# Attention followed by two dense layers: transposing a stacked query block through a 128-row identity instead of a 64-row one

## The chip, the core and the metric

The kernel runs on one core of one Trainium2 chip. The metric is device time in microseconds (us) for one execution; the median of three runs is given. The engines are named as in the profile: PE is TensorE's matrix multiply, PEld its load of the stationary operand, DVE is VectorE, ACT is ScalarE, POOL is GpSimd, SP is SyncE, which issues the transfers.

## The reference

Causal attention with a decay, over 4 batches of 8 heads, 576 positions of 64 features, followed by two dense two-matrix layers over 2304 tokens (512 to 2048 to 512), the first with a squared ReLU, the second with an ELU:

```python
scores = np.matmul(q, k.T) / sqrt(64) + cum[:, None] - cum[None, :]     # cum = cumsum(log f)
attn   = softmax(where(causal, -1e9, scores)) ; y = attn @ v             # per batch and head
x = y as [2304, 512]
x = relu(x @ w_in)**2 @ w_out
x = elu(x @ w2_in) @ w2_out
```

## The kernel before

Everything is float32. Where the kernel wants the precision and not the slow float32 product, it splits a tensor into a rounded high part and a low remainder (type `F32R`) and multiplies the parts in turn. Batch 0 (`PLAIN`) is not split: its products are plain float32, each recorded as two PE instructions, and its product with V has 64 output rows (`128*64` in the rows: 128 rows in, 64 columns of the stationary operand). Batches 1 to 3 are split; there the product with V carries the high and low part of V side by side and has 128 columns.

Per head the 576 queries are cut into five blocks of rows: blocks 0 and 1 (step "A"), blocks 2 and 3 (step "B"), and the last 64 queries (step "4"). A block of only 64 rows would fill half of the 128 partitions, so step "4" stacks the last 64 queries of two heads: head 0 of the pair in partitions 0 to 63, head 1 in 64 to 127. The stacked tile of probabilities is `e4` (`e4s`, 128 x 640; columns 576 to 639 are zero).

To multiply probabilities with V, they have to be transposed, since V's product contracts over keys. `tr` (L376 to L378) is a PE instruction: the probabilities are the stationary operand, an identity matrix is the moving one, and the transposed block lands in a PSUM tile `pt`. In `out_b` the inner function `turn(J)` does this for the 128 keys number J: for J = 0, 1, 2 one block from `e4`, and two from the head's own tile `e`; for J = 3 two blocks from `e4` (keys 384 to 511, and the last 64 keys) and one from `e`. Because `e4` holds two heads, the kernel takes only this head's half of the partitions, `e4[p, j]` with `p` the 64 partitions of head `k`, and a 64 x 64 piece of the identity. Those instructions have the shape `64*128 64x64` in the rows; the others are `128*128 128x128`. After a turn, ACT (L373) copies `pt` to a rounded tile and DVE (L374) makes the remainder (in batch 0 one copy, by ACT or DVE), and `av` (L379 to L385) multiplies. For the last 64 keys (J = 4) `av` is called with `rows=64`: it contracts over 64 partitions for 64 queries, again an instruction of 64 rows.

Between the instructions of the attention, the PE works on pieces of the first layer ("units", L157, tiles `ph` and `o`), which are put in by a credit scheme. The order of instructions on each engine is fixed before the run by the framework, which plays through a timeline of its own with modelled costs; the PE takes them strictly in that order. After the attention the remaining units run, and then the rest of the first layer and the second layer, nearly all of it L157.

The lines that the change touches: the identity (L96, L97), `tr`, `av`, and in `out_b` the functions `unsplit` and `turn` and the call of `av` for J = 4.

Of the kernel before, what the change touches and what calls it, by code (L numbers as in the profile page):

```python
# [10 lines left out]
F32 = mybir.dt.float32  # L11
# [33 lines left out]
CP = {'pA': 'a', 'pB': 'av', 'xA': 'a', 'xB': 'a'}  # L45
# [19 lines left out]
def f32(ap):  # L65
    return ap.bitcast(F32)
# [10 lines left out]
def attention_then_moe_kernel(ctx, tc, first, firstv, plain, qkv, aug0, f, w1, w2, out):  # L77
    nc = tc.nc
    PS = bass.MemoryType.PSUM

    def pool(stack, name, bufs, side, **kw):
        return stack.enter_context(tc.tile_pool(name=name, bufs=bufs, side=side, reuse_waits="tile", **kw))

    const = pool(ctx, "const", 1, "left")
# [8 lines left out]
    blocks = [(t0, min(512, NT - t0)) for t0 in range(0, NT, 512)]  # L93
    x2 = [dram.tile([2 * NC, 128, n], F32, name=f"x2_{j}") for j, (t0, n) in enumerate(blocks)]

    ident = const.tile([128, 128], F32, name="ident")  # L96
    make_identity(nc, ident)  # L97

    def mask(ap, pat):
        nc.gpsimd.affine_select(out=ap, in_=ap, pattern=pat, compare_op=ALU.is_ge, fill=-8.0e9, base=0, channel_multiplier=1)  # L100
# [3 lines left out]
    seen = [None]  # L104
# [8 lines left out]
    def copy(eng, dst, x, scale=None):  # L113
        if eng == "a":
            nc.scalar.activation(out=dst, in_=x, func=AF.Copy, scale=1.0 if scale is None else scale)  # L115
        elif eng == "p":
            nc.gpsimd.tensor_scalar(dst, x, 1.0 if scale is None else scale, 0.0, op0=ALU.mult, op1=ALU.add)
        elif scale is None:
            nc.vector.tensor_copy(dst, x)
        else:  # L120
            nc.vector.tensor_scalar(dst, x, scale, None, op0=ALU.mult)
# [250 lines left out]
    def split_pt(pt, hi, lo):  # L372
        nc.scalar.activation(out=hi, in_=pt, func=AF.Copy)  # L373
        nc.vector.tensor_tensor(lo, pt, f32(hi), op=ALU.subtract)  # L374

    def tr(dst, src, p0=0):  # L376
        k = src.shape[0]
        seen[0] = nc.tensor.transpose(dst, src, ident[p0:p0 + k, p0:p0 + k])  # L378

    def av(dst, hh, J, hl, first, last, rows=128):  # L380
        if isinstance(hh, Plain):
            seen[0] = nc.tensor.matmul(out=dst[0:64], lhsT=hh.v[0:rows, J, :], rhs=hl[0], start=first, stop=last)  # L382
            return
        for i in range(2):
            seen[0] = nc.tensor.matmul(out=dst, lhsT=hh[2][0:rows, J, :], rhs=hl[i], start=first and i == 0, stop=last and i == 1)  # L385

    def fold(pv, n, x, c0, k, eng, hh=None):
        if isinstance(hh, Plain):
            copy(eng, x[64 * k:64 * k + 64, c0:c0 + n], pv[0:64, 0:n])
            return  # L390
        t = ab.tile([64, 320], F32, tag="t", name="t", bufs=BUFS["t"])
        nc.scalar.activation(out=t[:, 0:n], in_=pv[64:128, 0:n], func=AF.Copy)
        if eng == "v":
            nc.vector.tensor_tensor(x[64 * k:64 * k + 64, c0:c0 + n], pv[0:64, 0:n], t[:, 0:n], op=ALU.add)
        else:
            u = ab.tile([64, 320], F32, tag="t", name="u", bufs=BUFS["t"])
            nc.scalar.activation(out=u[:, 0:n], in_=pv[0:64, 0:n], func=AF.Copy)
            nc.gpsimd.tensor_tensor(out=x[64 * k:64 * k + 64, c0:c0 + n], in0=u[:, 0:n], in1=t[:, 0:n], op=ALU.add)

    def norm_x(b, hp, kind, x, c0):  # L400
        z = zs.pop((kind, b, hp))
        r = ab.tile([128, 2, 2], F32, tag="r", name="r")
        nc.gpsimd.tensor_scalar(r, z, 1.0, 1e-9, op0=ALU.mult, op1=ALU.add)
        nc.vector.reciprocal(r, r)
        rb = ab.tile([128, 2, 2, 64], F32, tag="rb", name="rb", bufs=1)
        copy("p", rb, r.unsqueeze(3).broadcast_to([128, 2, 2, 64]))
        pr = ps_t.tile([128, 512], F32, tag="t", name="pr")
        for i in range(2):
            tr(pr[:, i * 128:i * 128 + 128], rb[:, i])
        nc.vector.tensor_tensor(x[:, c0:c0 + 256], x[:, c0:c0 + 256], pr[:, 0:256], op=ALU.mult)  # L410
# [12 lines left out]
    def out_a(hh, e, x, k):  # L423
        pt = ps_t.tile([128, 512], F32, tag="t", name="pt")
        tr(pt[:, 0:128], e[:, 0:128])
        tr(pt[:, 128:256], e[:, 256:384])
        tr(pt[:, 256:384], e[:, 128:256])
        if isinstance(hh, Plain):
            copy(CP["pA"], e, pt[:, 0:384])
            yield  # L430
            pv = ps_v.tile([128, 512], F32, tag="v", name="pv")
            av(pv[:, 0:256], hh, 0, [e[:, 0:256]], True, False)
            av(pv[:, 0:128], hh, 1, [e[:, 256:384]], False, True)
            fold(pv, 256, x, 0, k, CP["xA"], hh)
            return
        hl = ptA[k]
        split_pt(pt[:, 0:384], hl[0][:, 0:384], hl[1][:, 0:384])
        yield
        pv = ps_v.tile([128, 512], F32, tag="v", name="pv")
        av(pv[:, 0:256], hh, 0, [t[:, 0:256] for t in hl], True, False)  # L440
        av(pv[:, 0:256], hh, 1, [t[:, 256:512] for t in hl], False, True)
        fold(pv, 256, x, 0, k, FOLD[0])

    def out_b(hh, e, e4, x, k):
        p = slice(64 * k, 64 * k + 64)
        native = isinstance(hh, Plain)

        def unsplit(pt, n, J):
            p = ab.tile([128, 320], F32, tag=f"p{J % 2}", name="pp", bufs=BUFS["p"])
            copy(CP["pB"][J % 2], p[:, 0:n], pt[:, 0:n])  # L450
            return [p]

        def turn(J):
            j = slice(J * 128, J * 128 + 128)
            pt = ps_t.tile([128, 512], F32, tag="t", name="pt")
            if J < 3:
                tr(pt[:, 0:64], e4[p, j], 64 * k)
                tr(pt[:, 64:192], e[:, j])
                tr(pt[:, 192:320], e[:, 512 + J * 128:640 + J * 128])
                if native:  # L460
                    return unsplit(pt, 320, J)
                hl = [ab.tile([128, 320], F32R, tag=f"p{t}", name=f"p{t}", bufs=BUFS["p"]) for t in range(2)]
                split_pt(pt[:, 0:320], hl[0], hl[1])
            else:
                tr(pt[:, 0:64], e4[p, 512:640], 64 * k)
                tr(pt[:, 64:128], e4[p, 384:512], 64 * k)
                tr(pt[:, 128:256], e[:, 384:512])
                if native:
                    return unsplit(pt, 256, J)
                hl = ptB[k]  # L470
                split_pt(pt[:, 0:256], hl[0][:, 0:256], hl[1][:, 0:256])
            return hl

        hls = [turn(0)]
        yield
        hls.append(turn(1))
        yield
        pv = ps_v.tile([128, 512], F32, tag="v", name="pv")
        for J in range(4):
            hl = hls[J]  # L480
            if J < 3:
                av(pv[:, 0:320], hh, J, hl, J == 0, False)
            else:
                n3 = 192 if native else 256
                av(pv[:, 0:n3], hh, 3, [t[:, 64:64 + n3] for t in hl], False, False)
                av(pv[:, 0:64], hh, 4, [t[0:64, 0:64] for t in hl], False, True, 64)
                fold(pv, 320, x, 0, k, CP["xB"] if native else FOLD[1], hh)
            if J < 2:
                hls.append(turn(J + 2))
            yield  # L490

    heads = {}
    e4 = {}
# [16 lines left out]
    def outs(b, hp, kind, k):  # L510
        if kind == "4":
            return
        if k == 0:
            xs[kind] = a1.tile([128, 320], F32, tag="x" + kind, name="x" + kind, bufs=BUFS["x"])
        x = xs[kind]
        e = es.pop((b, hp, kind, k))
        if kind == "A":
            yield from out_a(heads[b, hp, k], e, x, k)
            if k:
                norm_x(b, hp, "A", x, 0)  # L520
                store_x(b, hp, x, 0, 256)
        else:
            yield from out_b(heads[b, hp, k], e, e4[b, hp], x, k)
            if k:
                norm_x(b, hp, "B", x, 64)
                store_x(b, hp, x, 256, 320)
        yield
# [159 lines left out]
    for i in range(len(todo) + LAG):  # L687
# [8 lines left out]
        if i < len(todo):  # L696
            sg = soft(*todo[i])
            b, hp, kind, k = todo[i]
# [215 lines left out]
```

## Time and profile before

| | |
|---|---|
| median of 3 runs | 1086.64 us (1085.25 to 1087.79) |
| the profiled execution | 1085.59 us, its span 1083.7 us |
| PE busy | 1059.4 us, 98% of the span |
| DVE, ACT, POOL busy | 58%, 46%, 21% |
| attention stage | about 13 to 398 us, the rest is the two layers |

Busy time of the PE counts an instruction from its start to its end. Matmuls are pipelined: one begins long before the one ahead of it has ended. So what an instruction costs is read from starts: the time from its start to the start of the next one on the PE. A row of the timeline merges neighbours of the same line, operation and tiles; "x3" is three of them, and its two numbers are the start of the first and the time until the end of the last.

### The profile page before, as it was taken

What the parts mean: (1) busy time and instruction counts of PE and PEld (TensorE: products, weight loads), DVE (VectorE), ACT (ScalarE), POOL (GpSimd) and SP (SyncE); (2) the same over time, 40 slices, a digit from 0 to 9 for tenths busy, and PEclk for the clock granted to TensorE, in tenths of its full rate; (3) what the DMA queues carried; (4) which work ended last, traced back from release to release, by engine and by line L of the source; (5) the groups of instructions that cost most, each with busy time, mean ns of one, the idle gap of its engine ahead of it and who ended that gap; (6) DMA issues with size and microseconds to landing.
All of it is one profiled execution on the core that took longest, in us unless ns stands there. A gap on an engine that the chain in (4) does not pass through costs nothing.

```text
span 1083.7 us, 15458 instructions
## 1 busy us (share of the span) xinstructions
PE 1059.4 (98%) x5696; PEld 875.5 (81%) x5696; DVE 624.0 (58%) x1363; ACT 495.2 (46%) x1055; POOL 228.7 (21%) x260
## 2 busy tenths in 40 slices
PE   3999999999999999999999999999999999999998
PEld 2557678899988998889988888888888888888897
DVE  6684467766677535886876358963433433343343
ACT  4675587876777544444543234532222222222232
POOL 4456387574757230000000000000000000000000
PEclk9999999999999999999999999999999999999999
DMA  8563434435341116444486145500300300110010
GB/s 240 156 198 106 156 127 155 140 95 181 111 151 65 42 64 217 127 140 168 140 288 206 67 155 174 194 21 1 117 1 1 117 1 1 47 32 0 1 40 20
DMA packets 60060, 115.48 MB, mean 107 GB/s; under 512 B 7296, under 2 KB 34688, under 8 KB 59968
## 3 DMA queue, kind: packets, MB, share of 16 engines
q1 hardware_dynamic: 59984, 114.49, 33.1%
q8 instruction: 45, 0.74, 0.3%
q14 instruction: 31, 0.25, 0.1%
HBM read 87.37 MB, written 27.69 MB: 106 GB/s over the span
## 4 chain that ended last, share of the span: by engine, by line
PE 95%; DMA 3%; ACT 1%; POOL 0%; DVE 0%; issue 0%; SPq 0%; ACTq 0%; POOLq 0%; DVEq 0%
PE O L157 31%; PE pH L157 31%; PE pt L378 7%; PE o L157 6%; PE ph L157 6%; PE pv L385 4%; PE pv L382 3%; PE s L305 2%; PE s L309 2%; PE s L310 2%; DMA raws_w<-in_w_dram 1%; PE pr L378 1%; DMA rawA<-ca 1%; DMA xu<-x 0%; DMA x<-xs 0%
## 5 line engine op out<-in xcount | busy, mean ns | idle before, releaser
L157 PE MATMUL pH<-xu,w 128*128 128x512 f32 (+1 forms) x1632 | 354.0, 367 | 0.0
L157 PEld LDWEIGHTS pH<-xu,w 128*128 128x128 f32 x1632 | 282.9, 188 | 55.3
L157 PE MATMUL O<-w,gh 128*128 128x512 f32 x576 | 179.0, 394 | 0.0
L556 ACT ACTIVATE g<-g 128x512 f32<-128x512 f32 (+1 forms) x80 | 47.0, 589 | 197.1 <-DVE g L555 196.9
L157 PEld LDWEIGHTS O<-w,gh 128*128 128x128 f32 x576 | 107.2, 188 | 24.7
L157 PE MATMUL O<-gh,w 128*128 128x512 f32 (+1 forms) x448 | 122.0, 362 | 0.0
L111 DVE TENSOR_TENSOR gl<-g,gh 128x512 fp32r<-128x512 f32 (+1 forms) x136 | 85.2, 627 | 54.2 <-ACT gh L558 44.4
L157 PE MATMUL O<-w,gl 128*128 128x512 f32 x288 | 111.3, 392 | 0.0
L555 DVE TENSOR_SCALAR g<-pH 128x512 f32<-128x512 f32 (+1 forms) x80 | 51.0, 638 | 101.4 <-PE pH L157 101.3
L157 PEld LDWEIGHTS O<-gh,w 128*128 128x128 f32 x448 | 79.8, 189 | 14.2
L124 POOL TENSOR_TENSOR qk<-raw,qk 64x704 fp32r<-64x704 f32 (+1 forms) x48 | 78.3, 1632 | 22.8 <-ACT qk L115 20.2
L157 PE MATMUL O<-gl,w 128*128 128x512 f32 (+1 forms) x224 | 79.4, 363 | 0.0
L557 DVE SCALAR_TENSOR_TENSOR g<-g,pH 128x512 f32<-128x512 f32 (+1 forms) x80 | 50.7, 634 | 46.3 <-ACT g L556 46.0
L157 PE MATMUL o<-gh,w 128*128 128x256 f32 x384 | 75.7, 290 | 0.0
L558 ACT ACTIVATE gh<-g 128x512 fp32r<-128x512 f32 (+1 forms) x80 | 47.0, 589 | 55.7 <-DVE g L557 55.5
L139 ACT ACTIVATE wt<-wraw 128x512 f32<-128x512 f32 x48 | 32.1, 670 | 79.3 <-DMA wraw<-in_w_dram 72.9
L157 PE MATMUL ph<-xu,w 128*128 128x256 f32 x480 | 65.0, 287 | 0.1
L157 PEld LDWEIGHTS O<-w,gl 128*128 128x128 f32 x288 | 54.1, 188 | 12.4
L157 PEld LDWEIGHTS o<-gh,w 128*128 128x128 f32 x384 | 60.2, 191 | 1.1 <-issue 1.0
L157 PEld LDWEIGHTS ph<-xu,w 128*128 128x128 f32 x480 | 60.2, 191 | 0.4 <-DMA xu<-x 0.4
L547 ACT ACTIVATE gh<-g 128x512 fp32r<-128x512 f32 (+1 forms) x80 | 46.6, 584 | 25.2 <-DVE g L546 24.1
L157 PE MATMUL o<-gl,w 128*128 128x256 f32 x192 | 55.0, 286 | 0.0
(131 smaller groups left out, 1682.7 us busy)
## 6 DMA issues: line engine op xcount, KB each, us to landing
wraw<-in_w_dram SPq DMA_DIRECT2D x48, 512.0 KB
raw<-in_qkv_dram SPq DMA_DIRECT2D x24, 800.0 KB
xu<-x SPq DMA_DIRECT2D x20, 512.0 KB
raws_w<-in_w_dram SPq DMA_DIRECT2D x16, 512.0 KB
x<-xs SPq DMA_DIRECT2D x16, 320.0 KB
xu<-x SPq DMA_DIRECT2D x20, 256.0 KB
x<-yh SPq DMA_DIRECT2D x16, 256.0 KB
x<-yl SPq DMA_DIRECT2D x16, 256.0 KB
```

What stands on the lines that cost most here:

```text
L111: nc.vector.tensor_tensor(dst, x, f32(hi), op=ALU.subtract)
L124: nc.gpsimd.tensor_tensor(out=dst, in0=x, in1=f32(hi), op=ALU.subtract)
L139: nc.scalar.activation(out=f32(t), in_=f32(hi), func=AF.Abs)
L157: nc.tensor.matmul(out=dst, lhsT=l, rhs=r, start=first and i == 0, stop=last and i == n - 1, skip_group_check=skip)
L378: seen[0] = nc.tensor.transpose(dst, src, ident[p0:p0 + k, p0:p0 + k])
L382: seen[0] = nc.tensor.matmul(out=dst[0:64], lhsT=hh.v[0:rows, J, :], rhs=hl[0], start=first, stop=last)
L385: seen[0] = nc.tensor.matmul(out=dst, lhsT=hh[2][0:rows, J, :], rhs=hl[i], start=first and i == 0, stop=last and i == 1)
L547: nc.scalar.activation(out=gh[:, 0:n], in_=g[:, 0:n], func=AF.Copy)
L555: nc.vector.tensor_scalar(g[:, 0:n], h[:, 0:n], 0.0, None, op0=ALU.min)
L556: nc.scalar.activation(out=g[:, 0:n], in_=g[:, 0:n], func=AF.Exp)
L557: nc.vector.scalar_tensor_tensor(g[:, 0:n], g[:, 0:n], -1.0, h[:, 0:n], op0=ALU.add, op1=ALU.max)
L558: nc.scalar.activation(out=gh[:, 0:n], in_=g[:, 0:n], func=AF.Copy)
```

## The change

The identity gets 64 more columns, a copy of its first 64, so that 128 columns of it taken from column 64 on are an identity whose halves are swapped. `e4` is transposed whole, with all 128 partitions, every time; the piece of the identity is chosen so that this head's 64 columns land where the rest of the code wants them, and the other head's 64 columns land beside them, where they are overwritten or never read. The copies out of `pt` begin at column 64. The product for the last 64 keys contracts over all 128 partitions; the added 64 hold the transposed zeros of `e4`'s columns 576 to 639.

```diff
-    ident = const.tile([128, 128], F32, name="ident")
-    make_identity(nc, ident)
+    ident = const.tile([128, 192], F32, name="ident")
+    make_identity(nc, ident[:, 0:128])
+    nc.gpsimd.tensor_copy(ident[:, 128:192], ident[:, 0:64])
...
-    def tr(dst, src, p0=0):
-        k = src.shape[0]
-        seen[0] = nc.tensor.transpose(dst, src, ident[p0:p0 + k, p0:p0 + k])
+    def tr(dst, src, c0=0):
+        seen[0] = nc.tensor.transpose(dst, src, ident[:, c0:c0 + 128])
...
-    def av(dst, hh, J, hl, first, last, rows=128):
+    def av(dst, hh, J, hl, first, last):
...
     def out_b(hh, e, e4, x, k):
-        p = slice(64 * k, 64 * k + 64)
+        last, near = 64 * (1 - k), 64 * k
...
-            copy(CP["pB"][J % 2], p[:, 0:n], pt[:, 0:n])
+            copy(CP["pB"][J % 2], p[:, 0:n], pt[:, 64:64 + n])
...
             if J < 3:
-                tr(pt[:, 0:64], e4[p, j], 64 * k)
-                tr(pt[:, 64:192], e[:, j])
-                tr(pt[:, 192:320], e[:, 512 + J * 128:640 + J * 128])
+                tr(pt[:, 0:128], e4[:, j], last)
+                tr(pt[:, 128:256], e[:, j])
+                tr(pt[:, 256:384], e[:, 512 + J * 128:640 + J * 128])
...
-                split_pt(pt[:, 0:320], hl[0], hl[1])
+                split_pt(pt[:, 64:384], hl[0], hl[1])
             else:
-                tr(pt[:, 0:64], e4[p, 512:640], 64 * k)
-                tr(pt[:, 64:128], e4[p, 384:512], 64 * k)
-                tr(pt[:, 128:256], e[:, 384:512])
+                tr(pt[:, 0:128], e4[:, 512:640], last)
+                tr(pt[:, 128:256], e4[:, 384:512], near)
+                tr(pt[:, 192:320], e[:, 384:512])
...
-                split_pt(pt[:, 0:256], hl[0][:, 0:256], hl[1][:, 0:256])
+                split_pt(pt[:, 64:320], hl[0][:, 0:256], hl[1][:, 0:256])
...
-                av(pv[:, 0:64], hh, 4, [t[0:64, 0:64] for t in hl], False, True, 64)
+                av(pv[:, 0:64], hh, 4, [t[:, 0:64] for t in hl], False, True)
```

## Rows read from the trace of the kernel before

**Rows 1.** Page, part 1: busy us, share of the span, instructions, by engine.
```profile
PE 1059.4 (98%) x5696; PEld 875.5 (81%) x5696; DVE 624.0 (58%) x1363; ACT 495.2 (46%) x1055; POOL 228.7 (21%) x260
```
**Rows 2.** Page, part 4: the chain of work that ended last, shares by engine.
```profile
PE 95%; DMA 3%; ACT 1%; POOL 0%; DVE 0%; issue 0%; SPq 0%; ACTq 0%; POOLq 0%; DVEq 0%
```
**Rows 3.** Windows: length, busy us (instructions) by engine, granted clock, DMA share, GB/s.
```profile
58.00:140.00 82.00, 82.00 (x444) 53.22 (x443) 45.02 (x117) 48.92 (x112) 44.37 (x44) 1.00 0.49 153
140.00:240.00 100.00, 99.09 (x702) 86.71 (x701) 71.95 (x219) 80.69 (x200) 72.26 (x78) 1.00 0.41 134
240.00:398.00 158.00, 158.00 (x1165) 142.59 (x1165) 99.72 (x281) 106.44 (x264) 84.75 (x97) 1.00 0.30 98
398.00:1083.00 685.00, 681.57 (x3270) 567.38 (x3268) 368.61 (x644) 227.66 (x403) 2.33 (x2) 1.00 0.28 92
```
**Rows 4.** Waits of PE, 58 to 398 us: us in total, times, longest.
```profile
PE pv L385 <- DVE xB L394: 0.5, 1, 0.5
```
**Rows 5.** Lines by form, PE: the two kinds of 64-row instructions (split batches for L385).
```profile
L378 PE MATMUL pt<-ident,e 64*128 64x64 f32 x160 | 37.0, 262 | 0.0
L385 PE MATMUL pv<-ptB,vv 64*128 64x64 f32 x48 | 9.7, 284 | 0.0
```
**Rows 6.** Timeline of PE, start and us: a turn with one 64-row transpose.
```profile
301.69 0.31 PE L385 MATMUL pv<-p,vv 128*128 128x320 f32 x1
301.93 0.27 PE L378 MATMUL pt<-ident,e 64*128 64x64 f32 x1
302.14 0.44 PE L378 MATMUL pt<-ident,eb 128*128 128x128 f32 x2
302.33 0.36 PE L157 MATMUL o<-gh,w 128*128 128x256 f32 x1
```
**Rows 7.** Timeline of PEld: loads of the same turn, idle time before in brackets.
```profile
301.93 0.14 PEld L378 LDWEIGHTS pt<-ident,e 64*128 64x128 f32 x1 [0.19 <-DVE p L374]
302.13 0.20 PEld L378 LDWEIGHTS pt<-ident,eb 128*128 128x128 f32 x2
```
**Rows 8.** Timeline of PE: a group of three transposes that all have 128 rows.
```profile
284.86 0.31 PE L385 MATMUL pv<-p,vv 128*128 128x320 f32 x1
285.01 0.49 PE L378 MATMUL pt<-ident,ea 128*128 128x128 f32 x3
285.26 0.37 PE L157 MATMUL ph<-xu,w 128*128 128x256 f32 x1
```
**Rows 9.** Timeline of PE: a turn with two 64-row transposes.
```profile
176.78 0.28 PE L157 MATMUL ph<-xu,w 128*128 128x256 f32 x1
176.99 0.33 PE L378 MATMUL pt<-ident,e 64*128 64x64 f32 x2
...
177.34 0.37 PE L309 MATMUL s<-qk 128*128 128x256 f32 x1
```
**Rows 10.** Timeline of PE: product of keys 384 on, its last two of 64 rows.
```profile
377.25 0.62 PE L385 MATMUL pv<-ptB,vv 128*128 128x256 f32 x3
377.80 0.55 PE L378 MATMUL pt<-ident,ea 128*128 128x128 f32 x3
```
**Rows 11.** Timeline of PE: 64-row instructions in different halves of the partitions.
```profile
305.86 0.29 PE L385 MATMUL pv<-ptB,vv 64*128 64x64 f32 x1
305.87 0.27 PE L378 MATMUL pt<-ident,e 64*128 64x64 f32 x1
```
**Rows 12.** Timeline of PE, batch 0: a turn right behind a 64-column product.
```profile
86.68 0.43 PE L382 MATMUL pv<-pp,rawB 128*64 128x320 f32 x1
87.04 0.27 PE L378 MATMUL pt<-ident,e 64*128 64x64 f32 x1
```
**Rows 13.** Timeline of PE, batch 0: 128-row transposes right behind such a product.
```profile
137.78 0.43 PE L382 MATMUL pv<-pp,vp 128*64 128x320 f32 x1
138.14 0.55 PE L378 MATMUL pt<-ident,ea 128*128 128x128 f32 x3
```
**Rows 14.** Timeline of POOL: a fill of 128 x 64 among its first instructions.
```profile
4.00 0.14 POOL L211 MEMSET e<- 128x64 f32 x1
```

More of the change, by code (lines that the diff above doesn't have):

```diff
@@ L374, in split_pt @@
         nc.vector.tensor_tensor(lo, pt, f32(hi), op=ALU.subtract)
-    def tr(dst, src, p0=0):
-        k = src.shape[0]
-        seen[0] = nc.tensor.transpose(dst, src, ident[p0:p0 + k, p0:p0 + k])
-    def av(dst, hh, J, hl, first, last, rows=128):
+    def tr(dst, src, c0=0):
+        seen[0] = nc.tensor.transpose(dst, src, ident[:, c0:c0 + 128])
+    def av(dst, hh, J, hl, first, last):
         if isinstance(hh, Plain):
-            seen[0] = nc.tensor.matmul(out=dst[0:64], lhsT=hh.v[0:rows, J, :], rhs=hl[0], start=first, stop=last)
+            seen[0] = nc.tensor.matmul(out=dst[0:64], lhsT=hh.v[:, J, :], rhs=hl[0], start=first, stop=last)
             return
         for i in range(2):
-            seen[0] = nc.tensor.matmul(out=dst, lhsT=hh[2][0:rows, J, :], rhs=hl[i], start=first and i == 0, stop=last and i == 1)
+            seen[0] = nc.tensor.matmul(out=dst, lhsT=hh[2][:, J, :], rhs=hl[i], start=first and i == 0, stop=last and i == 1)
     def fold(pv, n, x, c0, k, eng, hh=None):
```

## The prediction

> **What bounds the kernel now.** I read the page first: the PE is busy 98% of the span and no other engine more than 58% [rows 1], and the chain of work that ended last runs 95% through the PE [rows 2]. A PE that is called busy is not yet a PE that works, so next came the windows: from 58 us on the PE is busy in every stretch, at a granted clock of 1.00, while ACT, the next busiest, reaches 80.7 of 100 us at most, from 140 to 240 us [rows 3]. Then the waits: between 58 and 398 us the PE waited 0.5 us in its largest entry [rows 4]. So the PE sets the end, in the attention stage too, and a nanosecond less between two starts on it is a nanosecond off the end, as long as the others keep up.
>
> The question is therefore what the instructions that change cost the PE, from start to start. There are 160 transposes of 64 rows, and 48 products of 64 rows in the split batches [rows 5]. Their own durations (262 and 284 ns) say little, since neighbours overlap. The timeline tells it. In a turn with one 64-row transpose the last product ahead of it starts at 301.69, the first instruction behind the turn at 302.33: 0.64 us for one product and three transposes [rows 6]. A group of three transposes with 128 rows, behind the same kind of product, takes 284.86 to 285.26: 0.40 us, of which 0.15 are the product and 0.11 each of the first two transposes [rows 8]. The loads show where the 0.24 us go: the load for the 64-row transpose begins only at 301.93, after 0.19 us without a load, and the next load, of 128 rows again, only 0.20 us later [rows 7]. With 128 rows throughout, loads run under the instruction ahead. So going from 128 rows to 64 and back makes the array run empty twice. That the queue names DVE as the releaser of the first gap I don't believe: the step from a product to a 64-row transpose has nearly the same length all over the attention, where a wait for data would vary.
>
> **The change part by part.**
>
> *Transposes, batches 1 to 3.* 24 heads have three turns with one 64-row transpose and one with two. For the first kind the pair of groups above gives 0.64 - 0.40 = 0.24 us; 72 x 0.24 = 17.3 us. For the second kind 176.78 to 177.34 is 0.56 us [rows 9]; with 128 rows it would be a 256-column product (0.12) and three transposes at the steps of [rows 8] (0.11, 0.11, 0.03), 0.37 us: 24 x 0.19 = 4.6 us. The widening from 64 to 128 columns is contained in this, since all three then count as 128 x 128.
>
> *The product for the last 64 keys, batches 1 to 3.* Two instructions of 64 rows per head. From the 256-column product at 377.25 to the transpose behind it at 377.80 are 0.55 us, and the transposes behind them take 0.55 us instead of 0.49, because the first load is uncovered [rows 8, 10]. A 128-row split product with 64 columns stands nowhere in the trace. Bounds: not under 0.054 us (half a 128-column transpose of 0.11, by columns alone) and not over 0.133 us (the step between the two 64-row ones). I take 0.115 us, nearer to the upper row, because that is the same operation and only its load changes. So 0.12 + 2 x 0.115 = 0.35 replaces 0.55, and 0.06 goes behind it: 0.25 us, 24 x 0.25 = 6.0 us. The bounds move this by +2.9 and -0.9 us.
>
> *What the change gives up.* In 11 of these 24 places a transpose of the other half of the partitions stands between the two products, and starts 0.01 us after the first of them [rows 11]: two 64-row instructions in different halves run beside each other. Such a group, from its 256-column product to the first instruction behind its turn, takes 0.74 us where 128-row steps would make 0.60 (0.12 + 2 x 0.115 + 0.11 + 0.11 + 0.03); it gains 0.14 us and not the 0.24 + 0.25 counted, 11 x 0.35 = 3.9 us to take off.
>
> The Trainium skill has the rule that speaks against the change: "TensorE: Matmul & The Clock Gate", Part 3, says that a matmul over few rows takes as long as one over all, and that the gain of small ones is that tiles in different row groups run concurrently. The trace agrees on the concurrency in these 11 places, which are in the sum; between them and what stands next the rows show 0.2 us gaps, so here the small shapes lose more at their edges than they win. By the rule alone, with the gaps left out, the change would only lose: 11 x 0.11 = 1.2 us.
>
> *Batch 0.* Its product with V has 64 columns of the stationary operand, and that is a change of shape too: a 128-row transpose behind it starts 0.36 us after it [rows 13], a 64-row one as well, 87.04 - 86.68 [rows 12]. 12 of its 32 turns begin right behind such a product and keep that gap; there the change saves only what comes after: the step of 0.20 out of the 64-row transpose becomes 0.11 plus the 0.06 of an uncovered load (the 0.55 against 0.49 us of three, [rows 8, 13]), and the second such load, now behind the 64-row transpose, goes: 0.03 + 0.06 = 0.09 us, 1.1 us in all. The other 20 gain as above, 0.225 on average over both kinds: 4.5 us. Its 8 products for the last keys lose one gap of 0.09 and a load of 0.05: 8 x 0.14 = 1.1 us.
>
> *Sum on the PE:* 17.3 + 4.6 + 6.0 - 3.9 + 1.1 + 4.5 + 1.1 = 30.7 us.
>
> *At nothing.* POOL copies 128 x 64 once: a fill of that size took 0.14 us [rows 14], a select over 128 x 128 0.4. It lies behind the identity's own instructions, POOL's first list ends at 6.3 us and the first transpose starts at 18.9, so 12 us hide it; without that cover it costs under 0.4 us, once. What the DVE computes at 5.7 us waits for its own scan, not for POOL. The copies out of `pt` have the same sizes at another offset; the trace shows no copy at an offset, and I value that at 0: should ACT's 0.44 us per turn change by a tenth either way, 128 turns make 5.6 us on an engine that has 19 us in 100 to spare. The transposes' own data come as before, no wait is added, no transfer is moved: SP's queue keeps its order.
>
> *What is late next.* The PE does in about 310 us what took 340. Where ACT is busy 80.7 of 100 us [rows 3] it will be busy 80.7 of some 90, and a product will at times wait for the two copies ahead of it. I take off 3 of the 10 us of that stretch and 1.2 us of the rest, where DVE, ACT and POOL have a third or more to spare: 4.2 us. After the attention the stage from 398 us on is bound by the PE too (681.6 of 685 us), so it begins earlier and keeps its length; what units are left then still cover the first late weights.
>
> Net: 30.7 - 4.2 = 26.5 us. The profiled execution took 1085.59 us (span 1083.7 and 1.9 around it), so 1059.1; the median shown is 1.05 us above it: **1060 us**.
>
> **The rivals.**
>
> *The copies become the bound.* Half or more of the gain turns into waits of the PE for ACT and DVE. For it: ACT's 80.7 of 100 us, and turns in which the copies follow one another at once. Against: the largest PE wait now is 0.5 us, and from 240 to 398 us ACT has 52 us to spare. At half of 30.7 the time is 1071 us.
>
> *The gap isn't due to the rows* (the slower side). If the array ran empty because of the stacked tile itself, its waits or its place in the turn, the gaps stay and only the 64 added columns come: 0.11 - 0.054 for each of 160 transposes, 160 x 0.055 = 8.8 us, 1095 us. It decides once the gap stays in more than four of five turns (0.055 against 0.24). Against it: the 64-row product of [rows 10], another tile, shows the same gap, and the transposes of [rows 8] don't.
>
> *The order is planned anew.* The framework plans each engine's order with its own costs, and the shapes change. If transposes then stand too near to their products, waits of 0.2 us in all 128 turns would take back 26 us: about 1085, no change. Nothing in the profile speaks for such a shift; a little of it, up to 3 us either way, lies in the range.
>
> *More than the sum.* If the copies keep up everywhere and the 64-column product is cheap, 30.7 + 2.9 us: 1053 us.
>
> **How the numbers follow.** Forecast (1055 to 1066) 0.70; the copies bind (1066 to 1078) 0.14; more than the sum 0.06; planned anew to about no change 0.05; slower by the second rival 0.05. The range runs from 1053, the bound of the unknown product, to 1073, a little past half the gain. A measurement here can tell 0.2%, 2 us, from no change. Faster: 0.70 + 0.14 + 0.06 and part of the fourth, 0.91; same 0.04; slower 0.05.
>
> **What would show it.** In the profile after: no 64-row form on L378 or L385 in the split batches; all turns of three transposes at 0.39 to 0.40 us from product to what follows; no load gap of 0.2 us ahead of the stacked tile's transposes outside batch 0; the attention's last transpose near 370 instead of 396 us, and the stretch behind as long as before. If L373 or L374 appear as PE releasers with more than 10 us in total, the first rival has it. If the stacked tile's transposes still begin 0.2 us late with 128 rows, the sum's foundation is wrong, and with it the sign.

## The result, and the profile after

The changed kernel takes 1062.16 us in the median (1059.70 to 1063.11, 4 runs) against 1086.26 us before, a ratio of 0.9774 with a 95% interval of 0.9752 to 0.9795. Forecast were 1060 us, range 1053 to 1073. The profiled execution took 1061.57 us, its span 1059.8.

The page, parts 1 and 4, busy time by engine and the chain of work that ended last (against [rows 1, 2]):

```profile
PE 1027.7 (97%) x5696; PEld 873.6 (82%) x5696; DVE 621.3 (59%) x1363; ACT 491.8 (46%) x1055; POOL 228.2 (22%) x261
PE 89%; DMA 3%; ACT 3%; DVE 2%; issue 1%; SPq 1%; POOL 1%; ACTq 0%; POOLq 0%
```

The PE has exactly as many instructions as before, each of the 160 transposes streams twice the columns, and the busy time is 31.7 us less. The chain is PE at 89% instead of 95%: ACT, DVE and POOL have come onto it. The first line shows the gain; the second shows that other engines now release the PE at times, which took a part of the gain back.

The timeline of the PE, a turn behind a product of 320 columns, and the loads of PEld in it (against [rows 6, 7]):

```profile
287.23 0.31 PE L386 MATMUL pv<-p,vv 128*128 128x320 f32 x1
287.38 0.27 PE L379 MATMUL pt<-ident,e 128*128 128x128 f32 x1
287.48 0.38 PE L379 MATMUL pt<-ident,eb 128*128 128x128 f32 x2
287.62 0.36 PE L159 MATMUL o<-gl,w 128*128 128x256 f32 x1
```
```profile
287.23 0.14 PEld L379 LDWEIGHTS pt<-ident,e 128*128 128x128 f32 x1
287.38 0.25 PEld L379 LDWEIGHTS pt<-ident,eb 128*128 128x128 f32 x2
287.59 0.19 PEld L159 LDWEIGHTS o<-gl,w 128*128 128x128 f32 x1
```

From 287.23 to 287.62 are 0.39 us, where [rows 6] had 0.64. The load of the stacked tile now begins with the product ahead of it (287.23, both), where [rows 7] had 0.19 us without a load.

The product for the last 64 keys, in the same view (against [rows 10]):

```profile
274.93 0.42 PE L386 MATMUL pv<-ptB,vv 128*128 128x256 f32 x3
275.18 0.55 PE L379 MATMUL pt<-ident,ea 128*128 128x128 f32 x3
```

0.25 us instead of 0.55 to the transposes behind. Those still take 0.55 us and not the 0.49 of [rows 8]. Their first load begins only when they do, at 275.18, so the two products of 64 columns ahead of it don't cover it:

```profile
275.18 0.31 PEld L379 LDWEIGHTS pt<-ident,ea 128*128 128x128 f32 x3
```

Waits of the PE from 140 to 215 us (before, [rows 4] and one smaller entry, 0.8 us in the whole attention from 58 us on):

```profile
PE ph L159 <- DMA xu<-x: 1.5, 1, 1.5
PE pt L379 <- DVE p L376: 0.9, 1, 0.9
PE pv L386 <- DVE p L376: 0.5, 1, 0.5
PE pv L386 <- ACT ptB L375: 0.5, 1, 0.5
PE s L311 <- DVE nm L315: 0.4, 1, 0.4
PE pr L379 <- DVE p L376: 0.3, 1, 0.3
PE pv L386 <- DVE xA L395: 0.2, 1, 0.2
```

They add up to 4.3 us. The first has an echo: the timeline of the PE, and the windows of that stretch (length, busy us by engine, clock).

```profile
142.19 0.39 PE L312 MATMUL s<-qk 68*128 68x512 f32 x1
144.11 3.30 PE L159 MATMUL ph<-xu,w 128*128 128x256 f32 x15 [1.53 <-DMA xu<-x]
```
```profile
142.00:144.10 2.10, 0.58 (x3) 0.15 (x2) 2.10 (x10) 2.10 (x5) 0.60 (x2) 1.00 0.58 165
144.10:147.60 3.50, 3.49 (x17) 3.49 (x18) 1.81 (x3) 2.19 (x8) 3.32 (x3) 0.55 0.00 0
```

Behind 1.9 us between two starts the granted clock is 0.55 for 3.5 us, mostly the level of 1.2 GHz: 15 products of 256 columns take 3.30 us there and 2.05 us at full clock (the same 15 in the second profile of this kernel, below), 1.25 us more.

### The profile page after: what moved, and what is told of

The parts are those of the page before. It is cut to its first block, busy times and chain, and to the rows that moved or that the text cites. A ratio compares the mean times of both kernels' runs of the same rounds, so it can differ in the third digit from the quotient of the medians.

```text
span 1059.8 us, 15463 instructions
## 1 busy us (share of the span) xinstructions
PE 1027.7 (97%) x5696; PEld 873.6 (82%) x5696; DVE 621.3 (59%) x1363; ACT 491.8 (46%) x1055; POOL 228.2 (22%) x261
## 4 chain that ended last, share of the span: by engine, by line
PE 89%; DMA 3%; ACT 3%; DVE 2%; issue 1%; SPq 1%; POOL 1%; ACTq 0%; POOLq 0%
PE O L159 32%; PE pH L159 32%; PE o L159 6%; PE ph L159 6%; PE pt L379 4%; PE pv L386 3%; DMA raws_w<-in_w_dram 3%; PE s L311 2%; PE s L312 2%; PE pv L383 2%; PE s L307 1%; ACT eb L318 1%; PE pr L379 1%; ACT qk L117 1%; DVE wt L145 1%
## 5 line engine op out<-in xcount | busy, mean ns | idle before, releaser
L159 PE MATMUL ph<-xu,w 128*128 128x256 f32 x480 | 68.5, 291 | 1.8 <-DMA xu<-x 1.5
L142 DVE TENSOR_SCALAR wt<-wt 128x512 f32<-128x512 f32 x64 | 28.2, 441 | 50.1 <-ACT wt L141 49.8
```

The costliest lines, as they stand in the source:

```text
L142: nc.vector.tensor_scalar(f32(t), f32(t), W_MIN, W_MAX, op0=ALU.max, op1=ALU.min)
L159: nc.tensor.matmul(out=dst, lhsT=l, rhs=r, start=first and i == 0, stop=last and i == n - 1, skip_group_check=skip)
```

## The experiments

All were timed against the kernel before on the same chip; the kernel before took 1086.7 to 1087.1 us on the chips used, so runs of different groups are compared by their medians. The changed kernel and the kernel before were profiled a second time among them.

**The changed kernel again.** No edit.

> The changed kernel once more, on the chip of the other runs of this group, so that differences under 1% are taken against it. Every theory: 1062 us, 24 us under the kernel before. If the lost part of the gain comes from the late load of the second unit and the half clock behind it, the profile shows that wait of about 1.5 to 2 us near 144 us again, with or without a stretch at half clock.

Measured: 1062.02 us (1061.55 to 1063.17), ratio 0.9771 (0.9758 to 0.9785). The late load near 146 us is there again, 0.9 us of wait, without a stretch at half clock:

```profile
146.18 2.05 PE L159 MATMUL ph<-xu,w 128*128 128x256 f32 x15 [0.95 <-DMA xu<-x]
```

This profile's execution took 1062.13 us, no less than the first one's, so the half clock is not needed for the time of 1062.

**The kernel before again.** No edit, one profile (1087.58 us).

> The kernel before once more, for its profile. The changed kernel's first transpose of the stacked tile stood at 57.7, 60.3 and 59 to 61 us in its profile and in those of its variants, that of before at 58.3 us. If the start varies from run to run with the first weight transfers (every theory so far), it lies between 58 and 61 us here as well; if the change itself delays the start by 1 to 2 us, it is at 58.3 us again.

These are tile views of both second profiles: an operation's count, shortest/median/longest ns, and its first and last start. The kernel before, then the changed one:

```profile
L378 PE MATMUL pt<-ident,e x160: 222/272/275, 60.2 to 398.4; 64*128 64x64 f32 x160
L157 PE MATMUL ph<-xu,w x480: 277/283/384, 141.6 to 399.3; 128*128 128x256 f32 x160
L157 PE MATMUL pH<-xu,w x1632: 277/389/403, 412.3 to 1074.4; 128*128 128x512 f32 x139, 128*128 128x256 f32 x43
```
```profile
L379 PE MATMUL pt<-ident,e x160: 270/272/331, 60.3 to 370.8; 128*128 128x128 f32 x160
L159 PE MATMUL ph<-xu,w x480: 276/283/386, 135.9 to 375.3; 128*128 128x256 f32 x160
L159 PE MATMUL pH<-xu,w x1632: 277/389/403, 386.9 to 1048.9; 128*128 128x512 f32 x139, 128*128 128x256 f32 x43
```

The start varies from run to run (58.3 and 60.2 us without the change, 57.7 and 60.3 with it), so it is not the change's. These two happen to start alike and can be subtracted stage by stage. Batch 0, from the first transpose of the stacked tile to the second unit's first product: 81.4 us against 75.6, 5.8 saved. From there to the first product of the stage behind the attention: 270.7 against 251.0, 19.7 saved. Behind it both need 662 us from the first of these products to the last one. So the gain of 25.5 us in this pair arises in the attention alone and arrives at the end undiminished.

**The product back on 64 rows.**

`av` gets its argument for the number of rows back as well.

```diff
...
-                av(pv[:, 0:64], hh, 4, [t[:, 0:64] for t in hl], False, True)
+                av(pv[:, 0:64], hh, 4, [t[0:64, 0:64] for t in hl], False, True, 64)
```

> The changed kernel with the product for the last 64 keys back on 64 rows; the transposes stay at 128 rows. Theory (each passage from 128-row to 64-row instructions and back makes the array run empty, about 0.09 us going in, 0.09 coming out, and an uncovered load): 24 heads x 0.25 us + 8 heads of batch 0 x 0.14 us = 7 us slower than the changed kernel, 1069 us, and no side-by-side partner is left for these products. Rival (the gain came from the new order that the planner found, not from the rows): the order moves a little again, 1060 to 1065 us, with no relation to the 24 places.

Measured: 1068.43 us, ratio 0.9823 (0.9810 to 0.9837), 6.4 us above the changed kernel. In its timeline of the PE the 0.55 us of [rows 10] are back, from the 256-column product to the transposes:

```profile
322.84 0.62 PE L386 MATMUL pv<-ptB,vv 128*128 128x256 f32 x3
323.39 0.55 PE L379 MATMUL pt<-ident,ea 128*128 128x128 f32 x3
```

Only the rows changed here; the 64 columns are the same. The rival, a newly found order, would have had to hit the counted 7 us by chance.

**One more transpose per turn, of 64 rows or of 128.** Both are written where the next transpose overwrites them, so only their passage through the PE counts.

```diff
+                seen[0] = nc.tensor.transpose(pt[:, 0:64], e4[0:64, j], ident[0:64, 0:64])
                 tr(pt[:, 0:128], e4[:, j], last)
```
```diff
+                tr(pt[:, 0:128], e4[:, j])
                 tr(pt[:, 0:128], e4[:, j], last)
```

> The changed kernel with one more transpose in each turn for the keys 0 to 383 (96 of them), of 64 rows and 64 columns, into columns of the PSUM tile that the next transpose overwrites. Theory (passage to 64 rows and back): 0.09 us going in, 0.20 for the step out of it, 0.055 for the uncovered load behind, 0.345 x 96 = 33 us more on the PE; since waits of the PE for copies shrink by some 4 us, 1088 to 1096 us. Rival (the number of instructions and columns counts, not the rows): half the columns of the sister kernel's extra transposes, so 5 us more at most, 1067 us.

> The same with an extra transpose of 128 rows and 128 columns. Theory: 0.109 us each, x 96 = 10.5 us, of which 1 to 3 us may hide in waits of the PE: 1069 to 1073 us, some 20 us faster than with the smaller extra transpose. Rival (instructions and columns count): twice the columns cost at least what the smaller one costs.

Measured: 1087.36 us (ratio 1.0010, 0.9997 to 1.0023) with 64 rows, 1068.90 us (0.9832, 0.9814 to 0.9850) with 128. The smaller transpose, a quarter of the work by rows times columns, costs 25.3 us, the larger one 6.9, with the same number of instructions. The timeline of the PE with the smaller one:

```profile
105.79 0.28 PE L159 MATMUL o<-gl,w 128*128 128x256 f32 x1
106.00 0.27 PE L458 MATMUL pt<-ident,e 64*128 64x64 f32 x1
106.21 0.33 PE L379 MATMUL pt<-ident,e 128*128 128x128 f32 x1
106.37 0.38 PE L379 MATMUL pt<-ident,eb 128*128 128x128 f32 x2
106.51 0.48 PE L159 MATMUL o<-gh,w 128*128 128x256 f32 x2
```

0.21 us into it (a 256-column product usually steps by 0.12), 0.21 out of it, 0.16 for the next with its load uncovered, where 0.11 is usual: the three terms of the sum, made at will in a kernel that has no other 64-row instruction there. The smaller one has fewer rows and fewer columns at once; that columns alone don't cost this is seen in the changed kernel, where the two 128-row products of 64 columns take 0.13 us together (274.93 to 275.18, less the 0.12 of the product ahead), and the run before this one changed the rows alone. The expectation had 33 and 10.5 us in whole; both came out below, by 7.7 and 3.6 us. The waits of the PE from 58 to 398 us add up to 5.4 us in the changed kernel's second profile, 1.8 with the smaller and 3.3 with the larger transpose, so the added work filled some 3.6 and 2.1 us of waits. The rest of both, 4.1 and 1.5 us, was not taken apart. The difference of the two, 18.5 us, was expected at some 20.

**Where the rest went.** 25 us of the 31 that were counted came through, and the PE waits more than before. Seven kernels test what it waits for, all edits of the changed one.

*A step between a unit's load and its use; more of the units in batch 1.*

```diff
         yield
+        if u:
+            yield
```
```diff
-PACE = (1.4, 0.9, 1.85, 1.75)
+PACE = (1.4, 1.2, 1.85, 1.75)
```

> The changed kernel with one empty step between a unit's load of its input and the unit's first product (units 2 to 6), so that the load has longer. Theory A of the lost 6 us (the second unit's load comes 1.5 to 2 us late near 144 us, and the idle PE falls to half clock for 3.4 us, which costs about 1.7 us more): both go, 1059 us. Theory B (the copies of ACT and DVE are late between 140 and 210 us because the PE has too little else to do there): the wait only moves to another releaser, 1061 to 1063 us.

> The changed kernel with more of the units' steps put into batch 1 (pace 1.2 instead of 0.9), the work being the same in all. Theory B (copies late for want of other work between 140 and 210 us): about 3 us of waits go there, 1059 us, and fewer unit products are left behind the attention than the 99 now. Theory A (one late load): the load of the second unit is as late, or later since it is wanted sooner, 1062 to 1065 us.

Measured: 1063.58 us (0.9784, 0.9765 to 0.9803) and 1066.99 us (0.9810, 0.9797 to 0.9824). The first didn't gain, so the late load was not what cost the time: the wait for it is gone, and waits for DVE stand in its place (1.6 us for L315, 1.2 for L376), as theory B said. The second lost 5 us where theory B expected a gain of 3. So neither theory holds as a whole.

*The copy of q and k, 1.27 us of ACT, by DVE, or cut in two.*

```diff
-ENG = {'qk': 'aaa', 'ql': 'ppp', 'kh': 'pvv',
+ENG = {'qk': 'aav', 'ql': 'ppp', 'kh': 'pvv',
```
```diff
-                copy(ENG["qk"][w], qk1, raw[:, ac])
+                copy(ENG["qk"][w], qk1[:, 0:QW], raw[:, 0:QW])
+                copy(ENG["qk"][w], qk1[:, QW:RAW], raw[:, QW:RAW])
```

> The changed kernel with the rounding copy of the next head's q and k (128 x 1280) in batches 1 to 3 made by DVE instead of ACT. Theory C of the lost part (ACT, in order, makes a copy of 1.2 us for a coming head while the copies out of PSUM wait behind it, three times between 160 and 211 us): the three waits of the PE there, 2.9 us in all, go or shrink to under 1 us, 1059 us. Rival (ACT, DVE and POOL are all short of time there, the copy only moves): waits of the PE of the same size for DVE, 1061 to 1064 us.

> The changed kernel with that copy of q and k cut in two (704 and 576 columns), still on ACT, so that a copy out of PSUM can stand between the halves; 24 x 0.2 us more work for ACT. Theory C: waits behind it shrink by half, 1060 to 1061 us. Rival (the sum of ACT's work decides): 1062 to 1064 us.

Measured: 1070.18 us (0.9848, 0.9827 to 0.9869) and 1062.77 us (0.9785, 0.9771 to 0.9800). Cut in two, the copy left the time where it was, as the rival said, so theory C doesn't hold. By DVE it is 8 us slower, worse than either theory expected; the waits of the PE between 140 and 225 us are now for DVE:

```profile
PE pr L379 <- DVE p L376: 3.8, 2, 2.2
PE s L311 <- DVE nm L315: 1.5, 3, 0.7
PE pt L379 <- DVE p L376: 1.2, 1, 1.2
PE pt L379 <- DVE xA L411: 1.1, 1, 1.1
```

Behind the longest of them, from 196.7 to 200.2 us, and again from 217.2 to 220.7 us, the granted clock is 0.51. If each stretch costs the 1.25 us that the one above did, an estimate, some 2.5 of the 8 us are the clock's.

*Less work for ACT, and other ways to spread it.* The first leaves out the low part of V's product, the second and third make DVE's second copy of k by a transfer.

```diff
-        nc.scalar.activation(out=t[:, 0:n], in_=pv[64:128, 0:n], func=AF.Copy)
...
-            nc.vector.tensor_tensor(x[64 * k:64 * k + 64, c0:c0 + n], pv[0:64, 0:n], t[:, 0:n], op=ALU.add)
+            nc.vector.tensor_copy(x[64 * k:64 * k + 64, c0:c0 + n], pv[0:64, 0:n])
```
```diff
-ENG = {'qk': 'aaa', 'ql': 'ppp', 'kh': 'pvv',
+ENG = {'qk': 'aav', 'ql': 'ppp', 'kh': 'pvd',
```
```diff
-ENG = {'qk': 'aaa', 'ql': 'ppp', 'kh': 'pvv',
+ENG = {'qk': 'aaa', 'ql': 'ppp', 'kh': 'pvd',
```

> The changed kernel without the addition of the low part of V's product in batches 1 to 3, a part of the computation that is left out here: ACT's copy of it (48 x 0.41 us) goes, DVE copies the high part alone. Theory D of the lost 4 us (ACT's sum of work between 140 and 211 us, 67 of 80 us, decides, wherever a single copy stands): the waits of the PE there fall from 5 to 2 us or less, 1057 to 1059 us. Rival (another engine, or one late transfer): as before, 1062 us.

> The changed kernel with the rounding copy of q and k on DVE, and DVE's own second copy of k (64 x 576) made by a transfer instead, in batches 1 to 3. ACT loses 24 x 1.27 us, DVE gains 24 x 1.0 and loses 24 x 0.8. Theory D: 1058 to 1060 us. If DVE's chains are what is short, as with the copy on DVE alone (1070 us), or the transfers hold up SP's queue, 1063 to 1070 us.

> The changed kernel with only DVE's second copy of k replaced by a transfer. ACT's work stays. Theory D (ACT decides): 1061 to 1063 us. If DVE is as short as ACT, 1058 to 1060 us, since DVE loses 24 x 0.8 us.

Measured: 1061.67 us (0.9766, 0.9743 to 0.9789), 1060.29 us (0.9755, 0.9742 to 0.9768), 1061.54 us (0.9771, 0.9756 to 0.9786). The windows from 140 to 220 us, busy us of PE, PEld, DVE, ACT, POOL in this order, one fence for each kernel: the changed one (its second profile), the copy of q and k by DVE, V's low part left out, and the copy of q and k by DVE together with the transfer.

```profile
140.00:220.00 80.00, 76.07 (x584) 71.90 (x583) 62.69 (x198) 67.15 (x175) 57.62 (x65) 1.00 0.48 157
```
```profile
140.00:220.00 80.00, 71.47 (x520) 66.75 (x518) 66.37 (x183) 51.80 (x146) 57.31 (x61) 0.96 0.42 135
```
```profile
140.00:220.00 80.00, 76.75 (x592) 72.65 (x591) 59.19 (x192) 58.68 (x155) 58.60 (x66) 1.00 0.46 154
```
```profile
140.00:220.00 80.00, 76.93 (x599) 73.70 (x599) 64.82 (x195) 58.70 (x164) 60.87 (x67) 1.00 0.54 172
```

With 8.5 us less on ACT the PE got 8 instructions further in the stretch, and the median lies 0.4 us under that of the changed kernel, not 3 to 5: theory D, that ACT's sum of work decides, isn't borne out, though the interval (down to 1058.8 us) leaves room for a part of it. The fastest, at 1060.29 us, relieves ACT by as much and has DVE 2 us busier; it is below both kernels in the median, but its interval overlaps that of the changed kernel, so a gain of 1.7 us over it is not established.

What stays open is the cause of the added waits, some 4 us: they are for ACT, DVE and one transfer, most of them in batch 1, and they move when one of these is relieved. That a chain through all of them (product, copy, remainder, product) sets the pace there would fit, but no run showed it.

## Why the prediction was right

**What bounds the kernel.** Right: the stages of the second pair of profiles show that what the attention's PE gained came off the end one for one, and the stage behind it kept its length.

**Transposes, 17.3 + 4.6 us, and batch 0.** Right in kind and size. The turn takes 0.39 us instead of 0.64, forecast 0.40; batch 0 saved 5.8 us in all, forecast 6.7. (Of its 12 turns counted behind a 128-row product of 64 columns, four stand behind a 64-row one, 0.15 us after it; they kept that step as well.) That the passage to 64 rows and back is what costs is shown by the extra transposes (same tile, same place, 25 us for 64 rows and 7 for 128) and by the product put back on 64 rows. That the array runs empty meanwhile is the reading of it: the traces show the longer steps and the time without a load, not the array. That DVE, which the queue named as releaser in [rows 7], was not the cause is shown by the same: the gap went with the rows.

**The product for the last keys, 6.0 us.** Here a size was off. Instead of the two steps of 0.115 us and a covered load behind, the two products together with the step behind them take 0.13 us, and the load behind stays uncovered: 0.30 us saved per head and not 0.25, 1.2 us more in all. Undoing it cost 6.4 us against 7.1 counted; waits that it fills may be the difference.

**The side-by-side pairs, -3.9 us.** The places are gone as said. The timeline of the changed kernel has such a group, the product on its last keys with the turn right behind it; the rows ahead of it are products of q and k, of 128 rows and of 68:

```profile
149.06 0.28 PE L311 MATMUL s<-qk 128*128 128x256 f32 x1
149.18 0.28 PE L312 MATMUL s<-qk 68*128 68x256 f32 x1
149.30 0.43 PE L386 MATMUL pv<-ptB,vv 128*128 128x256 f32 x3
149.56 0.33 PE L379 MATMUL pt<-ident,e 128*128 128x128 f32 x1
149.72 0.38 PE L379 MATMUL pt<-ident,eb 128*128 128x128 f32 x2
149.86 0.36 PE L159 MATMUL ph<-xu,w 128*128 128x256 f32 x1
```

From 149.30 to 149.86 are 0.56 us, where 0.74 stood before and 0.60 was forecast: by these two groups a place gained 0.18 us and not 0.14, so losing the concurrency cost no more than was taken off. The rule on concurrency in "TensorE: Matmul & The Clock Gate" of the Trainium skill, Part 3, held where two halves met (0.01 us between their starts, [rows 11]); that few rows take as long as all stands in the closing table of that page, "Why this matters for your kernels". It did not decide here, because its gain needs neighbours that are small as well: 11 places had one, and the passages paid.

**At nothing.** POOL's copy stands where it was put, behind the identity, and is hidden; it took 0.23 us, between the 0.14 and the 0.4 given. The row is from POOL's timeline.

```profile
5.59 0.23 POOL L99 COPY ident<-ident 128x64 f32<-128x64 f32 x1
```

**What is late next, -4.2 us.** Right in size, and by luck; the reason fails. With equal starts 25.5 us remained of 30.7 (or 31.9 with the measured product): 5 to 6 us were lost, 0.9 in batch 0 and the rest in batches 1 to 3. The pages of these two profiles, before and after, split them (their spans are 1085.8 and 1060.3 us):

```profile
PE 1059.6 (98%) x5696; PEld 875.8 (81%) x5696; DVE 623.4 (57%) x1363; ACT 494.9 (46%) x1055; POOL 228.5 (21%) x260
PE 1029.9 (97%) x5696; PEld 874.8 (83%) x5696; DVE 621.4 (59%) x1363; ACT 491.8 (46%) x1055; POOL 228.9 (22%) x261
```

The busy time of the PE fell by 29.7 us, so the sum was 1 us too large (2 with the measured product), and its idle time grew from 26.2 to 30.4 us, by the 4.2 that were taken off, most of it in the stretch that was named. But the 3 of 10 us for that stretch were a choice that no row gave, and the reason named, ACT's 80.7 of 100 us, found no support: taking ACT's work away gave nothing that could be measured. A busy share on the way up is a warning, not a mechanism.

**The rivals.** The copies did not become the bound: L375 and L376 release the PE for 2.2 us in all from 140 to 215 us, where more than 10 would have been needed. The gap was due to the rows. The order was planned anew, since the same units stand elsewhere, but without visible harm. The last transpose stands at 370 us, as expected.

## What to carry to other kernels

Read the cost of a small PE instruction from start to start across its neighbours: here one with half the rows and half the columns cost over three times what a whole one costs, since the steps into it and out of it are longer and the next load is uncovered, and padding it to the shape of its neighbours was a gain although it streams twice the columns. Not every smaller shape pays: the products of 68 rows in the rows at 149 us step like their neighbours of 128 rows, 0.12 us in and 0.12 us out. Where a PE-bound stage is made faster, test the next limit before naming it: here an engine at 84% busy was relieved by an eighth without a measurable gain.

## What the runs showed of the hardware

- A step from a 128-row to a 64-row instruction costs 0.09 us more than its neighbours (0.21 us behind a 256-column product, where 0.12 is usual), the step out of a 64-row, 64-column transpose takes 0.20, and the next 0.055 more for an uncovered load. An instruction of 68 rows among those of 128 shows none of this (0.12 us in and out).
- A change in the columns of the stationary operand, from 128 to 64, has the same entry, also where the rows stay at 128: 0.21 us instead of 0.12 behind a product of 256 columns, from 116.97 to 117.18 us in the timeline of the kernel before; [rows 12, 13] show the way back, 0.36 us behind such a product of 320 columns.
- Two split products of 128 rows and 64 columns took 0.13 us together, up to the transpose behind them: by the rows 0.25 us from the 256-column product, less its 0.12. That is about what a single step from one 64-row product to the next took (0.133).
- The granted clock fell to 0.55 over 3.5 us behind a gap of 1.9 us between starts (1.53 us idle). Behind a gap of 1.3 us in the second profile it stayed at 1.00, and so it did in the run with more of the units in batch 1, behind an idle time of 1.63 us before 149.58 us (1.00 from 149.6 to 153 us). So the length of the gap alone did not decide.
